# Decode attention with K in one load and the softmax in two parts

## The chip, the cores and the metric

The kernel runs on one core of one Trainium2 chip. The metric is the device time of one execution in microseconds (us). Engines: PE multiplies and transposes, DVE and ACT work element by element, POOL does small copies, SP issues the loads, and 16 DMA engines move the data. SBUF is the on-chip memory that the loads fill; names that start with ps are tiles in PSUM, where PE's results go. QK is K times q, PV is the weights P times V. The granted clock is the share of its full clock that PE was given.

## The reference

One decode step of a transformer block for two sequences. What matters here is the attention: 32 query heads in 4 groups, one K and one V cache per group and sequence (the reference repeats them for the 8 heads of a group).

```python
q = (h @ wq) ...                                    # one token per sequence
scores = einsum('bhqd,bhkd->bhqk', q, k) * Dh ** -0.5   # k: (2, 4, 32768, 128) bf16
p = softmax(scores)
o = einsum('bhqk,bhkd->bhqd', p, v)                 # v as large as k
x = x + ga * (o @ wo);  then an MLP of 1024 -> 3584 -> 1024
```

K and V are 67.1 MB each, the weights 44 MB. Each byte is loaded once.

## The kernel before

There are eight rounds, one for each pair of sequence and KV group. A round has 4 chunks of 8192 rows; a chunk is 8 groups of 8 tiles of 128 rows. SP issues every load on one queue, in order; a load waits until the buffer it overwrites has been read.

```python
def add_k(i, hf):    # two loads of 4 MB: chunks 0-1 and chunks 2-3, 32 KB a partition each
    add(("K", i, hf), [2, TPC * D], A_k_cache[...][hf], hf * 32 * KB, f"K{hf}")
def add_v(i):        # one load of 8 MB, 64 KB a partition
    add(("V", i), [NCH, TPC * D], A_v_cache[...], 64 * KB, "V")
...
for cc in range(NCH):
    for g8 in range(TPC // 8):
        tr(i, cc, g8)                 # PE: 8 transposes of K into PSUM; DVE or ACT copies them out
        pipe.append((i, cc, g8))
        if len(pipe) > PIPE: qk(*pipe.pop(0))     # PE: 8 products with q
        # last qk of a chunk: ACT copies the scores, DVE takes the maximum m1c
while pipe: qk(*pipe.pop(0))
softmax_1(); softmax_2(); softmax_3() # maximum over all 4 chunks and all partitions
for cc in range(NCH): exp(cc)         # DVE subtracts, ACT takes exp
for cc in range(NCH):
    part_sum(cc); pv(i, cc)           # DVE: row sums; PE: P times V into one bank
row_sums(); extract(); extract_2(i)   # the extraction: 1/sum, then the 4 blocks of the bank to "at"
```

## Time and profile before

| | before |
|---|---|
| time, median of 3 runs | 420.08 us (420.07 to 420.27) |
| HBM bytes read | 178.28 MB |
| rounds 1 to 7, from V landed to V landed | 38.61 to 38.71 us |
| busy share PE / DVE / ACT | 70 / 50 / 36 % |
| last load landed, end | 415.76, 418.70 us |

Before one asks what an engine does, one asks in which stretches the DMA is full; the prediction shows that table and the views that go with it. "V landed" means the semaphore event of V's load in the trace.

### The profile page before, as it was taken

The numbers are of one execution on the slowest core, as the hardware profiler recorded it, in microseconds if no ns is written. First come the engines' busy times: TensorE is split into PE (matmuls) and PEld (weight loads), VectorE is DVE, ScalarE is ACT, GpSimd is POOL, SyncE is SP. The second block draws the span as 40 slices with busy tenths as digits, with TensorE's granted clock in tenths as the row PEclk, the third lists the DMA queues.
The fourth block names the chain that finished last, engine by engine and source line by source line (L and its number), as shares of the span: only waits on it lengthen the run. The fifth ranks groups of instructions, "written<-read, shape, count | busy, mean of one in ns | idle before, by whom it ended". The sixth has DMA issues, their size and how long they took to land.

```text
span 418.7 us, 11609 instructions
## 1 busy us (share of the span) xinstructions
PE 291.0 (70%) x5183; PEld 231.3 (55%) x5183; DVE 209.6 (50%) x423; ACT 149.4 (36%) x179; POOL 6.8 (2%) x29
## 2 busy tenths in 40 slices
PE   1407449766996895699369957976995699564536
PEld 1104219762993794299149926962894399221214
DVE  1201105546677676467726664766477567620411
ACT  2000015533565364256405632643365166400100
POOL 3000000000000000000000000000000000000000
PEclk9999557986896997799589958986697889576585
DMA  9989999999999999999999999999999999899995
GB/s 373 450 380 449 448 404 493 398 406 446 441 432 429 423 451 429 419 454 457 391 435 476 407 416 448 438 438 426 438 438 426 416 460 457 377 448 428 424 427 249
DMA packets 5581, 178.42 MB, mean 426 GB/s; under 512 B 698, under 2 KB 706, under 8 KB 964
## 3 DMA queue, kind: packets, MB, share of 16 engines
q1 hardware_dynamic: 5572, 178.28, 98.8%
q8 instruction: 8, 0.13, 0.1%
q14 instruction: 1, 0.01, 0.0%
HBM read 178.28 MB, written 0.00 MB: 426 GB/s over the span
## 4 chain that ended last, share of the span: by engine, by line
DMA 71%; PE 24%; DVE 2%; issue 1%; ACT 1%; SPq 1%
DMA V<-in_A_v_cache_dram 39%; DMA wo<-in_A_wo_dram 10%; DMA K<-in_A_k_cache_dram 10%; PE psZ L584 10%; DMA w<-in_B_w_dram 9%; PE psKT L536 8%; DMA wmod<-in_w_mod_dram 4%; PE psS L548 1%; PE psZ L548 1%; PE psS L655 1%; PE psZ L729 1%; PE psZ L469 1%; ACT KT_sb L540 0%; PE psS L469 0%; DVE m1c L553 0%
## 5 line engine op out<-in xcount | busy, mean ns | idle before, releaser
L536 PE MATMUL psKT<-ident,K 128*128 128x128 bf16 x2048 | 163.1, 229 | 11.5 <-DMA K<-in_A_k_cache_dram 11.5
L540 ACT ACTIVATE KT_sb<-psKT 128x1024 bf16<-128x1024 bf16 x96 | 98.2, 1025 | 124.4 <-PE psKT L536 124.4
L542 DVE COPY KT_sb<-psKT 128x1024 bf16<-128x1024 bf16 x160 | 106.7, 688 | 61.6 <-PE psKT L536 61.2
L536 PEld LDWEIGHTS psKT<-ident,K 128*128 128x128 bf16 x2048 | 126.7, 102 | 13.0 <-DMA K<-in_A_k_cache_dram 12.7
L584 PE MATMUL psZ<-V,E_sb 128*32 128x512 bf16 x512 | 46.4, 541 | 23.2 <-DMA V<-in_A_v_cache_dram 20.0
L548 PE MATMUL psS<-qcur,KT_sb 128*128 128x8 bf16 x1024 | 44.7, 167 | 2.2 <-issue 2.2
L584 PEld LDWEIGHTS psZ<-V,E_sb 128*32 128x32 bf16 x512 | 18.7, 130 | 47.7 <-issue 38.8
L548 PE MATMUL psZ<-qcur,KT_sb 128*128 128x8 bf16 x1024 | 43.0, 167 | 2.2 <-issue 1.5
L548 PEld LDWEIGHTS psS<-qcur,KT_sb 128*128 128x128 bf16 x1024 | 40.0, 97 | 2.3 <-issue 2.3
L548 PEld LDWEIGHTS psZ<-qcur,KT_sb 128*128 128x128 bf16 x1024 | 37.9, 96 | 3.4 <-issue 1.6
L572 ACT ACTIVATE E_sb<-S_sb 128x512 bf16<-128x512 f32 x32 | 19.5, 630 | 29.6 <-DVE S_sb L570 29.6
L570 DVE TENSOR_TENSOR S_sb<-S_sb,gmb 128x512 f32<-128x512 f32 x32 | 20.0, 685 | 0.3
L576 DVE TENSOR_REDUCE rs<-E_sb 128x8 f32<-128x512 bf16 x32 | 19.7, 675 | 0.0
L469 PE MATMUL psS<-wmod,inT 128*32 128x512 bf16 x32 | 5.1, 624 | 16.2 <-DMA wmod<-in_w_mod_dram 16.2
L553 DVE TENSOR_REDUCE m1c<-psZ 128x8 f32<-128x512 f32 x16 | 11.1, 693 | 10.2 <-ACT S_sb L552 10.1
L595 DVE RECIPROCAL rinv<-psM 128x1 f32<-128x1 f32 x8 | 1.3, 168 | 27.7 <-PE psM L593 27.7
L605 PE MATMUL psM<-msum,hmat 128*128 128x128 f32 x16 | 4.2, 347 | 13.3 <-DVE msum L600 13.3
L559 PE MATMUL psM<-identf,m 128*8 128x128 f32 x16 | 4.3, 369 | 13.1 <-DVE m L556 13.1
L553 DVE TENSOR_REDUCE m1c<-psS 128x8 f32<-128x512 f32 x16 | 11.1, 693 | 3.2 <-ACT S_sb L552 3.1
L552 ACT ACTIVATE S_sb<-psZ 128x512 f32<-128x512 f32 x16 | 9.5, 595 | 7.5 <-PE psZ L548 7.5
L477 DVE COPY S_sb<-psS 128x512 f32<-128x512 f32 x1 | 0.7, 690 | 22.9 <-PE psS L469 22.9
L469 PEld LDWEIGHTS psS<-wmod,inT 128*32 128x32 bf16 x32 | 1.1, 132 | 19.3 <-DMA wmod<-in_w_mod_dram 18.0
(123 smaller groups left out, 167.5 us busy)
## 6 DMA issues: line engine op xcount, KB each, us to landing
K<-in_A_k_cache_dram SPq DMA_DIRECT2D x16, 4096.0 KB, 27.1
wq<-in_A_wq_dram SPq DMA_DIRECT2D x2, 4096.0 KB, 44.8
wo<-in_A_wo_dram SPq DMA_DIRECT2D x2, 4096.0 KB, 39.0
w<-in_B_w_dram SPq DMA_DIRECT2D x2, 3584.0 KB, 32.5
wmod<-in_w_mod_dram SPq DMA_DIRECT2D x1, 6144.0 KB, 29.8
w<-in_B_w_dram SPq DMA_DIRECT2D x3, 2048.0 KB, 37.8
wmod<-in_w_mod_dram SPq DMA_DIRECT2D x1, 4608.0 KB, 15.8
wmod<-in_w_mod_dram SPq DMA_DIRECT2D x1, 1536.0 KB, 6.0
```

The costliest lines, as they stand in the source:

```text
L469: pe(lambda e, w=it.view, k=k, kk=kk, ch=ch, n=n, q=q: e.matmul(bank[n][32 * q:32 * q + 32, :], lhsT=inT[:, k, :], rhs=w[:, kk, ch * 512:( ...
L536: pe(lambda e, kq=kq, jj=jj, w=kt, t=t: e.transpose(psKT[kq][:, jj * 128:(jj + 1) * 128], w[:, t, :], ident[:, :]), reads=[it.reg, "ident" ...
L540: act(lambda e, src=src: e.activation(KT_sb[g8][:, :, :], src, ACT.Copy), reads=[f"psKT{kq}"], writes=[f"KT_sb{g8}"], sem=f"ev{cc}_{g8}")
L542: dve(lambda e, src=src: e.tensor_copy(KT_sb[g8][:, :, :], src), reads=[f"psKT{kq}"], writes=[f"KT_sb{g8}"], sem=f"ev{cc}_{g8}")
L548: pe(lambda e, t=t, jj=jj: e.matmul(ps[:, t * HPG:(t + 1) * HPG], lhsT=KT_sb[g8][:, jj, :], rhs=qcur[:, :], start=True, stop=True), reads= ...
L552: act(lambda e: e.activation(Sc, ps.rearrange("p (t h) -> p h t", h=HPG), ACT.Copy), reads=[preg], writes=[f"S_sb_{cc}"], sem=f"sc{cc}")
L553: dve(lambda e: e.tensor_reduce(m1c[:, :, cc], ps.rearrange("p (t h) -> p h t", h=HPG), AX.X, ALU.max), reads=[preg], writes=[f"m1c{cc}"])
L559: pe(lambda e: e.matmul(psM[0:HPG, 0:128], lhsT=m1[:, :], rhs=identf[:, :], start=True, stop=True), reads=["m1", "identf"], writes=["psM"])
L570: dve(lambda e: e.tensor_tensor(Sc, Sc, gmb[:, :].unsqueeze(2).to_broadcast([128, HPG, TPC]), ALU.subtract), reads=[f"S_sb_{cc}", "gmb"], ...
L572: act(lambda e: e.activation(Ec, Sc.rearrange("p h (u t) -> p u h t", t=4), ACT.Exp, scale=SCALE), reads=[f"S_sb_{cc}"], writes=[f"E_sb_{c ...
L576: dve(lambda e: e.tensor_reduce(rs4[:, :, cc], Ec.rearrange("p u h t -> p h u t"), AX.XY, ALU.add), reads=[f"E_sb_{cc}"], writes=[f"rs4_{c ...
L584: pe(lambda e, t4=t4, tg=tg, q=q: e.matmul(psO[32 * q:32 * q + 32, :], lhsT=E_sb[:, tg // 4, :, :].rearrange("p h t -> p (h t)"), rhs=vt[: ...
```

## The change: intent and diff

The change wants PV to end sooner after K, and K to come in packets of 64 KB. Chunks 0 to 2 get their maximum and exponentials while chunk 3 is still being worked on; chunk 3 gets its own maximum, and both parts are weighted with exact factors. K now comes in one load of 8 MB into one buffer. To free that buffer early, DVE copies chunks 2 and 3 into a second 32 KB buffer. The small DVE steps are placed anew, and evacuation of transposed K alternates DVE and ACT.

```diff
-    def add_k(i, hf):
-        add(("K", i, hf), [2, TPC * D], ...[hf], hf * 32 * KB, f"K{hf}")
+    def add_k(i):                       # round 0: two loads ("K", "K2"); others: one
+        add(("K", i), [NCH, TPC * D], rows, 0, "K", view=kv)
...
-        it = need("K", i, cc // 2)
+        it = need("K", i)
+        kt = (kv[:, cc, :] if cc < 2 else kc[:, cc - 2, :])...
-        if EVAC_PATTERN[g8] == "act":   # 5 on DVE, 3 on ACT, the last on DVE
+        if g8 % 2:                      # 4 and 4, the last on ACT
+    def keep(i, n):                     # after groups (0,1), (0,3), (0,5), (1,1)
+        dve(lambda e: e.tensor_copy(kc[:, n // 2, lo:lo + 32 * D], kv[:, 2 + n // 2, lo:lo + 32 * D]), ...)
...
         if g8 == TPC // 8 - 1:
+            dve(... m1c: maximum of the chunk ...)
             act(... scores of the chunk to S_sb ...)
-            dve(... m1c ...)
...
-        softmax_1(); softmax_2(); softmax_3()
-        for cc in range(NCH): exp(cc)
-        for cc in range(NCH): part_sum(cc); pv(i, cc)
-        row_sums(); extract(); extract_2(i)
+        # inside chunk 3: max_1(), max_2(0), max_3(0)
+        exp(0); exp(1); [last qk]; exp(2)
+        pv(i, 0); max_2(1); part_sum(0); pv(i, 1); max_3(1); exp(3); weights()
+        pv(i, 2); part_sum(1); part_sum(2); weights_2(); extract(0)
+        pv(i, 3); part_sum(3); row_sums(); row_sums_2(); extract(1); extract_2(i)
```

(The places of the last weights in the buffers change too.)

More of the change, by code (lines that the diff above doesn't have):

```diff
@@ L34 @@
 RING = 160 * 1024
+KC_AT = 128 * 1024
 AHEAD = ("sc2", "sc3", "pk", "ac")
 WMOD_ITEMS = ((0, 1), (1, 4), (4, 8))
-W2_ITEMS = ((0, 8, 96), (8, 16, 112), (16, 24, 128), (24, 27, 144), (27, 28, 150))
-EVAC_PATTERN = ("dve", "act", "dve", "act", "dve", "dve", "act", "dve")
+W2_ITEMS = ((0, 8, 96), (8, 16, 112), (16, 24, 0), (24, 27, 16), (27, 28, 22))
+KEEP = {(0, 1): 0, (0, 3): 1, (0, 5): 2, (1, 1): 3}
 class Tracker:
@@ L211, in wait @@
             def wait(w):
+                if w[1] == 0:
+                    return eng.wait_ge(self.sem[w[0]], w[2])
                 eng.wait_ge(self.sem[w[0]], val[w[1:]] if w[1:] in val else it * w[1] + w[2])
@@ L250, in bass_adaLN_cond__gqa_block_cached__mixer_channel_mlp__decode_kernel @@
     T = Tracker(nc)
-    T.step["pe"], T.step["dve"] = 72, 14
+    T.step["pe"], T.step["dve"] = 74, 18
     def sb(name, shape, dtype=FP32):
@@ L305, in bass_adaLN_cond__gqa_block_cached__mixer_channel_mlp__decode_kernel @@
     diag = sb("diag", [HPG, HPG])
-    gmb = sb("gmb", [128, HPG])
+    gmb = sb("gmb", [128, 2, HPG])
+    mx = sb("mx", [128, HPG])
+    dw = sb("dw", [128, 2, HPG])
+    wt = sb("wt", [128, 2, HPG])
+    wh = sb("wh", [128, 2, HPG])
+    wp = sb("wp", [128, 2])
+    mkw = sb("mkw", [128, 2, 4])
     rowsum = sb("rowsum", [128, HPG])
-    rs4 = sb("rs4", [128, HPG, NCH])
+    rs4 = sb("rs4", [128, HPG, NCH - 1])
+    rs2 = sb("rs2", [128, 2, HPG])
     rinv = sb("rinv", [128, 1])
@@ L333, in bass_adaLN_cond__gqa_block_cached__mixer_channel_mlp__decode_kernel, with add @@
     KB = 1024
-    def add(key, shape, src, off, slot=None):
+    def add(key, shape, src, off, slot=None, sem=None, view=None):
         it = Item()
@@ L340, in add @@
         it.reg = f"it{it.n}"
-        it.sem = f"d_{slot or it.reg}"
-        it.view = views.get(slot)
+        it.sem = f"d_{sem or slot or it.reg}"
+        it.view = views.get(slot) if view is None else view
         if it.view is None:
@@ L349, in add @@
         by_key[key] = it
-    def add_k(i, hf):
-        add(("K", i, hf), [2, TPC * D], A_k_cache[i % 2, i // 2].rearrange("(p h c t) d -> h p c (t d)", h=2, c=2, p=128)[hf], hf * 32 * KB, f"K{hf}")
+    kv = nc.alloc_sbuf_tensor_at("kv", [128, NCH, TPC * D], BF16, offset=abase)
+    def add_k(i):
+        rows = A_k_cache[i % 2, i // 2].rearrange("(p c t) d -> p c (t d)", c=NCH, p=128)
+        if i:
+            add(("K", i), [NCH, TPC * D], rows, 0, "K", view=kv)
+            by_key["K2", i] = by_key["K", i]
+        else:
+            add(("K", i), [2, TPC * D], rows[:, 0:2, :], 0, sem="K", view=kv[:, 0:2, :])
+            add(("K2", i), [2, TPC * D], rows[:, 2:4, :], 32 * KB, sem="K2", view=kv[:, 2:4, :])
+            T.key("d_K2")
+            T.step["d_K2"] = 0
     def add_v(i):
@@ L364, in bass_adaLN_cond__gqa_block_cached__mixer_channel_mlp__decode_kernel @@
     for i in range(NBG):
-        add_k(i, 0)
-        add_k(i, 1)
+        add_k(i)
         add_v(i)
-    for m, off in enumerate((128, 0)):
+    for m, off in enumerate((0, 32)):
         add(("wo", m), [16, DM], A_wo[m * 2048:(m + 1) * 2048, :].rearrange("(p j) n -> p j n", j=16), off * KB)
     w1_v = B_w1.rearrange("(p k) n -> p k n", k=KT8)
-    for m, off in enumerate((32, 64)):
+    for m, off in enumerate((128, 64)):
         add(("w1", m), [4, F], w1_v[:, 4 * m:4 * m + 4, :], off * KB)
@@ L376, in bass_adaLN_cond__gqa_block_cached__mixer_channel_mlp__decode_kernel @@
     w2_of = {j: (m, j - j0) for m, (j0, j1, off) in enumerate(W2_ITEMS) for j in range(j0, j1)}
+    kc = nc.alloc_sbuf_tensor_at("kc", [128, 2, TPC * D], BF16, offset=abase + KC_AT)
     pos = [0]
@@ L384, in need @@
             old = [o.reg for o in stream[:cur.n] if o.off < cur.off + cur.nbytes and cur.off < o.off + o.nbytes]
+            if cur.n > by_key["V", NBG - 1].n and cur.off < KC_AT + 32 * KB and KC_AT < cur.off + cur.nbytes:
+                old += [f"kc{n}" for n in range(4)]
             if len(cur.view.shape) == 3:
@@ L516, in bass_adaLN_cond__gqa_block_cached__mixer_channel_mlp__decode_kernel @@
                reads=[f"qrow{n}", "ident"] + EREG, writes=["psM"], mark=(i == 3))
-    dve(lambda e: e.tensor_copy(qT[:, :, :], psM[:, 0:64].rearrange("p (b h) -> p b h", b=2)), reads=["psM"], writes=["qT"], sem="mo")
+    dve(lambda e: e.tensor_copy(qT[:, :, :], psM[:, 0:64].rearrange("p (b h) -> p b h", b=2)), reads=["psM"], writes=["qT"], sem="mo1")
     for name in AHEAD:
@@ L521, in bass_adaLN_cond__gqa_block_cached__mixer_channel_mlp__decode_kernel @@
         T.raw("pe", lambda e, name=name: e.sem_inc(T.sem[name], T.step.get(name, 1)))
+    T.wait("dve", writes=[it.reg for it in stream if it.key[0] in ("wmod", "wq")])
     T.wait("pe", reads=["ident", "identf", "onesf", "hmat"], writes=["psS0", "psS1", "psO", "psM"] + [f"psKT{q}" for q in range(NPKT)])
@@ L530, in tr @@
     def tr(i, cc, g8):
-        it = need("K", i, cc // 2)
-        kt = it.view[:, cc % 2, :].rearrange("p (t d) -> p t d", d=D)
+        it = need("K", i)
+        kt = (kv[:, cc, :] if cc < 2 else kc[:, cc - 2, :]).rearrange("p (t d) -> p t d", d=D)
+        k_reg = it.reg if cc < 2 else f"kc{2 * (cc - 2) + g8 // 4}"
         kq = g8 % NPKT
@@ L536, in tr @@
             pe(lambda e, kq=kq, jj=jj, w=kt, t=t: e.transpose(psKT[kq][:, jj * 128:(jj + 1) * 128], w[:, t, :], ident[:, :]),
-               reads=[it.reg, "ident"], writes=[f"psKT{kq}"], mark=(jj == 7))
+               reads=[k_reg, "ident"], writes=[f"psKT{kq}"], mark=(jj == 7))
         src = psKT[kq][:, :].rearrange("p (a n) -> p a n", a=8)
-        if EVAC_PATTERN[g8] == "act":
+        if g8 % 2:
             act(lambda e, src=src: e.activation(KT_sb[g8][:, :, :], src, ACT.Copy), reads=[f"psKT{kq}"], writes=[f"KT_sb{g8}"], sem=f"ev{cc}_{g8}")
@@ L542, in tr @@
             dve(lambda e, src=src: e.tensor_copy(KT_sb[g8][:, :, :], src), reads=[f"psKT{kq}"], writes=[f"KT_sb{g8}"], sem=f"ev{cc}_{g8}")
+    def keep(i, n):
+        it = need("K2", i)
+        lo = n % 2 * 32 * D
+        dve(lambda e: e.tensor_copy(kc[:, n // 2, lo:lo + 32 * D], kv[:, 2 + n // 2, lo:lo + 32 * D]), reads=[it.reg], writes=[f"kc{n}"], sem=f"kc{n}")
     def qk(i, cc, g8):
@@ L551, in qk @@
             Sc = S_sb[:, :, cc * TPC:(cc + 1) * TPC]
+            dve(lambda e: e.tensor_reduce(m1c[:, :, cc], ps.rearrange("p (t h) -> p h t", h=HPG), AX.X, ALU.max), reads=[preg], writes=[f"m1c{cc}"], sem=f"mc{cc}")
             act(lambda e: e.activation(Sc, ps.rearrange("p (t h) -> p h t", h=HPG), ACT.Copy), reads=[preg], writes=[f"S_sb_{cc}"], sem=f"sc{cc}")
-            dve(lambda e: e.tensor_reduce(m1c[:, :, cc], ps.rearrange("p (t h) -> p h t", h=HPG), AX.X, ALU.max), reads=[preg], writes=[f"m1c{cc}"])
@@ L555, in softmax_1 @@
-    def softmax_1():
-        dve(lambda e: e.tensor_reduce(m1[:, :], m1c[:, :, :], AX.X, ALU.max), reads=[f"m1c{cc}" for cc in range(NCH)], writes=["m1"], sem="m1")
-    def softmax_2():
-        pe(lambda e: e.matmul(psM[0:HPG, 0:128], lhsT=m1[:, :], rhs=identf[:, :], start=True, stop=True), reads=["m1", "identf"], writes=["psM"])
-        dve(lambda e: e.tensor_reduce(gm[:, :], psM[0:HPG, 0:128], AX.X, ALU.max), reads=["psM"], writes=["gm"], sem="gm")
-        dve(lambda e: e.tensor_scalar(diag[:, :], identf[0:HPG, 0:HPG], gm[:, 0:1], None, ALU.mult), reads=["identf", "gm"], writes=["diag"], sem="dg")
@@ L563, in softmax_3, with max_1, max_2 @@
-    def softmax_3():
+    def max_1():
+        dve(lambda e: e.tensor_reduce(m1[:, :], m1c[:, :, 0:NCH - 1], AX.X, ALU.max), reads=[f"m1c{cc}" for cc in range(NCH - 1)], writes=["m1"], sem="m1")
+    def max_2(part):
+        src, reg = (m1[:, :], "m1") if part == 0 else (m1c[:, :, NCH - 1], f"m1c{NCH - 1}")
+        pe(lambda e: e.matmul(psM[0:HPG, 0:128], lhsT=src, rhs=identf[:, :], start=True, stop=True), reads=[reg, "identf"], writes=["psM"])
+        dve(lambda e: e.tensor_reduce(gm[:, :], psM[0:HPG, 0:128], AX.X, ALU.max), reads=["psM"], writes=["gm"], sem=f"gm{part}")
+        dve(lambda e: e.tensor_scalar(diag[:, :], identf[0:HPG, 0:HPG], gm[:, 0:1], None, ALU.mult), reads=["identf", "gm"], writes=["diag"], sem=f"dg{part}")
@@ L564, in softmax_3, with max_3 @@
+    def max_3(part):
         pe(lambda e: e.matmul(psM[:, 128:128 + HPG], lhsT=onesf[0:HPG, :], rhs=diag[:, :], start=True, stop=True), reads=["onesf", "diag"], writes=["psM"])
-        dve(lambda e: e.tensor_copy(gmb[:, :], psM[:, 128:128 + HPG]), reads=["psM"], writes=["gmb"])
+        dve(lambda e: e.tensor_copy(gmb[:, part, :], psM[:, 128:128 + HPG]), reads=["psM"], writes=[f"gmb{part}"], sem=f"gb{part}")
     def exp(cc):
+        part = cc // (NCH - 1)
         Sc = S_sb[:, :, cc * TPC:(cc + 1) * TPC]
@@ L569, in exp @@
         Ec = E_sb[:, cc * TPC // 4:(cc + 1) * TPC // 4, :, :]
-        dve(lambda e: e.tensor_tensor(Sc, Sc, gmb[:, :].unsqueeze(2).to_broadcast([128, HPG, TPC]), ALU.subtract),
-            reads=[f"S_sb_{cc}", "gmb"], writes=[f"S_sb_{cc}"], sem=f"sb{cc}")
+        dve(lambda e: e.tensor_tensor(Sc, Sc, gmb[:, part, :].unsqueeze(2).to_broadcast([128, HPG, TPC]), ALU.subtract),
+            reads=[f"S_sb_{cc}", f"gmb{part}"], writes=[f"S_sb_{cc}"], sem=f"sb{cc}")
         act(lambda e: e.activation(Ec, Sc.rearrange("p h (u t) -> p u h t", t=4), ACT.Exp, scale=SCALE), reads=[f"S_sb_{cc}"], writes=[f"E_sb_{cc}"], sem=f"ex{cc}")
@@ L575, in part_sum, with weights, weights_2 @@
         Ec = E_sb[:, cc * TPC // 4:(cc + 1) * TPC // 4, :, :]
-        dve(lambda e: e.tensor_reduce(rs4[:, :, cc], Ec.rearrange("p u h t -> p h u t"), AX.XY, ALU.add), reads=[f"E_sb_{cc}"], writes=[f"rs4_{cc}"])
+        dst, reg = (rs4[:, :, cc], f"rs4_{cc}") if cc < NCH - 1 else (rs2[:, 1, :], "rs2_1")
+        dve(lambda e: e.tensor_reduce(dst, Ec.rearrange("p u h t -> p h u t"), AX.XY, ALU.add), reads=[f"E_sb_{cc}"], writes=[reg])
+    def weights():
+        dve(lambda e: e.tensor_tensor(mx[:, :], gmb[:, 0, :], gmb[:, 1, :], ALU.max), reads=["gmb0", "gmb1"], writes=["mx"])
+        dve(lambda e: e.tensor_tensor(dw[:, :, :], gmb[:, :, :], mx[:, :].unsqueeze(1).to_broadcast([128, 2, HPG]), ALU.subtract), reads=["gmb0", "gmb1", "mx"], writes=["dw"], sem="dw")
+        act(lambda e: e.activation(wt[:, :, :], dw[:, :, :], ACT.Exp, scale=SCALE), reads=["dw"], writes=["wt"], sem="wt")
+    def weights_2():
+        dve(lambda e: e.tensor_tensor(wh[:, :, :], wt[:, :, :], hsel[:, :].unsqueeze(1).to_broadcast([128, 2, HPG]), ALU.mult), reads=["wt", "hsel"], writes=["wh"])
+        dve(lambda e: e.tensor_reduce(wp[:, :], wh[:, :, :], AX.X, ALU.add), reads=["wh"], writes=["wp"])
+        dve(lambda e: e.tensor_tensor(mkw[:, :, :], mk4[:, :].unsqueeze(1).to_broadcast([128, 2, 4]), wp[:, :].unsqueeze(2).to_broadcast([128, 2, 4]), ALU.mult),
+            reads=["mk4", "wp"], writes=["mkw"])
     def pv(i, cc):
@@ L580, in pv @@
         vt = it.view[:, cc, :]
+        last = cc == NCH - 1
+        acc, reg = (psS[0], "psS0") if last else (psO, "psO")
         for t4 in range(TPC // 4):
@@ L583, in pv, with row_sums_2 @@
             q = t4 % 4
-            pe(lambda e, t4=t4, tg=tg, q=q: e.matmul(psO[32 * q:32 * q + 32, :], lhsT=E_sb[:, tg // 4, :, :].rearrange("p h t -> p (h t)"),
+            pe(lambda e, t4=t4, tg=tg, q=q: e.matmul(acc[32 * q:32 * q + 32, :], lhsT=E_sb[:, tg // 4, :, :].rearrange("p h t -> p (h t)"),
                                                     rhs=vt[:, t4 * 512:(t4 + 1) * 512],
-                                                    start=(cc == 0 and t4 < 4), stop=(cc == NCH - 1 and t4 >= TPC // 4 - 4),
+                                                    start=((last or cc == 0) and t4 < 4), stop=(cc >= NCH - 2 and t4 >= TPC // 4 - 4),
                                                     skip_group_check=True),
-               reads=[it.reg, f"E_sb_{cc}"], writes=["psO"], mark=(t4 == TPC // 4 - 1))
+               reads=[it.reg, f"E_sb_{cc}"], writes=[reg], mark=(t4 == TPC // 4 - 1))
     def row_sums():
-        dve(lambda e: e.tensor_reduce(rowsum[:, :], rs4[:, :, :], AX.X, ALU.add), reads=[f"rs4_{cc}" for cc in range(NCH)], writes=["rowsum"])
+        dve(lambda e: e.tensor_reduce(rs2[:, 0, :], rs4[:, :, :], AX.X, ALU.add), reads=[f"rs4_{cc}" for cc in range(NCH - 1)], writes=["rs2_0"])
+        dve(lambda e: e.tensor_tensor(wh[:, :, :], rs2[:, :, :], wt[:, :, :], ALU.mult), reads=["rs2_0", "rs2_1", "wt"], writes=["wh"])
+        dve(lambda e: e.tensor_tensor(rowsum[:, :], wh[:, 0, :], wh[:, 1, :], ALU.add), reads=["wh"], writes=["rowsum"])
         dve(lambda e: e.tensor_copy(rsum16[:, :, :, :], rowsum[:, :].unsqueeze(1).unsqueeze(3).to_broadcast([128, 2, HPG, 8])), reads=["rowsum"], writes=["rsum16"], sem="rs")
+    def row_sums_2():
         pe(lambda e: e.matmul(psM[:, 144:145], lhsT=rsum16.rearrange("p g h e -> p (g h e)"), rhs=onesf[:, 0:1], start=True, stop=True),
@@ L595, in row_sums, with extract @@
         dve(lambda e: e.reciprocal(rinv[:, :], psM[:, 144:145]), reads=["psM"], writes=["rinv"], sem="rv")
-    def extract():
-        dve(lambda e: e.tensor_scalar(msum[:, :], psO[:, 0:128], mk4[:, 0:1], None, ALU.mult), reads=["psO", "mk4"], writes=["msum"])
-        for q in range(1, 4):
-            dve(lambda e, q=q: e.scalar_tensor_tensor(out=msum[:, :], in0=psO[:, q * 128:(q + 1) * 128], scalar=mk4[:, q:q + 1], in1=msum[:, :],
-                                                      op0=ALU.mult, op1=ALU.add), reads=["psO", "mk4", "msum"], writes=["msum"], sem="mo" if q == 3 else None)
+    def extract(part):
+        acc, reg = ((psO, "psO"), (psS[0], "psS0"))[part]
+        for q in range(4):
+            if part == 0 and q == 0:
+                dve(lambda e: e.tensor_scalar(msum[:, :], acc[:, 0:128], mkw[:, 0, 0:1], None, ALU.mult), reads=[reg, "mkw"], writes=["msum"])
+            else:
+                dve(lambda e, q=q: e.scalar_tensor_tensor(out=msum[:, :], in0=acc[:, q * 128:(q + 1) * 128], scalar=mkw[:, part, q:q + 1], in1=msum[:, :],
+                                                          op0=ALU.mult, op1=ALU.add), reads=[reg, "mkw", "msum"], writes=["msum"], sem=f"mo{part}" if q == 3 else None)
     def extract_2(i):
@@ L624, in bass_adaLN_cond__gqa_block_cached__mixer_channel_mlp__decode_kernel @@
                 tr(i, cc, g8)
+                if (cc, g8) in KEEP:
+                    keep(i, KEEP[cc, g8])
                 pipe.append((i, cc, g8))
@@ L629, in bass_adaLN_cond__gqa_block_cached__mixer_channel_mlp__decode_kernel @@
                     qk(*pipe.pop(0))
+                if (cc, g8) == (3, 2):
+                    max_1()
+                if (cc, g8) == (3, 4):
+                    max_2(0)
+                if (cc, g8) == (3, 6):
+                    max_3(0)
+        exp(0)
+        exp(1)
         while pipe:
             qk(*pipe.pop(0))
-        softmax_1()
-        softmax_2()
-        softmax_3()
-        for cc in range(NCH):
-            exp(cc)
-        for cc in range(NCH):
-            part_sum(cc)
-            pv(i, cc)
+        exp(2)
+        pv(i, 0)
+        max_2(1)
+        part_sum(0)
+        pv(i, 1)
+        max_3(1)
+        exp(3)
+        weights()
+        pv(i, 2)
+        part_sum(1)
+        part_sum(2)
+        weights_2()
+        extract(0)
+        pv(i, 3)
+        part_sum(3)
         row_sums()
-        extract()
+        row_sums_2()
+        extract(1)
         extract_2(i)
```

## The prediction

> **What bounds the kernel now.** I started with the stretches of time, because they show at once whether one resource is full everywhere. I cut the span at the moments when the eight V loads land (from the landing events in the trace) and asked for busy time, granted PE clock, DMA share and rate of each stretch:
>
> ```profile
> core 0: us, PE busy (x) PEld busy (x) DVE busy (x) ACT busy (x) POOL busy (x), PEclk, DMA share, GB/s
> 0.00:6.76 6.76, 0.00 (x0) 0.00 (x0) 0.00 (x0) 1.28 (x1) 3.25 (x13) 1.00 0.84 321
> 6.76:62.41 55.65, 24.25 (x213) 11.56 (x213) 7.58 (x27) 4.15 (x6) 0.19 (x1) 0.80 1.00 432
> 130.31:168.97 38.66, 28.86 (x586) 24.52 (x586) 28.11 (x54) 20.62 (x26) 0.44 (x2) 0.85 1.00 434
> 168.97:207.66 38.69, 28.88 (x584) 24.50 (x584) 24.56 (x46) 18.03 (x22) 0.44 (x2) 0.85 1.00 434
> 362.37:413.23 50.86, 27.93 (x269) 13.00 (x269) 12.71 (x46) 3.82 (x7) 0.25 (x1) 0.67 1.00 427
> 413.23:418.70 5.47, 3.16 (x97) 2.81 (x97) 0.68 (x3) 0.00 (x0) 0.00 (x0) 0.50 0.25 100
> ```
>
> The reader should see the last two columns: a DMA share of 1.00 in every stretch between 6.76 and 413.23, at 427 to 434 GB/s, while in one round of 38.69 us PE is busy 28.88, DVE 24.56 and ACT 18.03. Only the first and last few us are not full of DMA. The page's queue lines say the same of the whole:
>
> ```profile
> q1 hardware_dynamic: 5572, 178.28, 98.8%
> HBM read 178.28 MB, written 0.00 MB: 426 GB/s over the span
> ```
>
> Next, the chain that ended last, to see which wait closes a round:
>
> ```profile
> 137.97 31.01 DMA V<-in_A_v_cache_dram
> 168.97 0.14 issue
> 169.11 5.76 PE psZ L584 x62
> 174.92 32.74 DMA V<-in_A_v_cache_dram
> 207.66 0.14 issue
> ```
>
> A round is a V load, then PV (L584), then the next V load. This alternation tempts one to call the PV part of the path: V is issued only when PV has freed its buffer. The sync engine's timeline corrects that:
>
> ```profile
> 150.11 10.67 SPq L389 DMA_DIRECT2D K<-in_A_k_cache_dram  x2
> 174.92 0.33 SPq L389 DMA_DIRECT2D V<-in_A_v_cache_dram  x1
> 188.40 10.68 SPq L389 DMA_DIRECT2D K<-in_A_k_cache_dram  x2
> ```
>
> V, issued at 174.92, lands at 207.66, so it is 32.7 us under way, though 8.39 MB at 434 GB/s need 19.3: it stands 13.4 us in the queue behind K. K, issued at 150.11, starts moving only when V has landed at 168.97, 18.9 us later. So the queue always holds work; PV could end 13 us later before the engines ran dry. And within that round the waits are compute waiting for data:
>
> ```profile
> PE psZ L584 <- DMA V<-in_A_v_cache_dram: 4.1, 1, 4.1
> PE psKT L536 <- DMA K<-in_A_k_cache_dram: 1.3, 1, 1.3
> ```
>
> Conclusion: the bound is the bytes. The rest is 1.75 us until the first packet and 2.9 us from the last landing (415.76) to the end (418.70).
>
> **What the Trainium skill says.** (1) "DMA: Bandwidth & Descriptors", section "Where 436 GB/s comes from": 16 ports give a ceiling of 435.2 GB/s. The trace agrees: 434 in a round. So 178.28 MB need at least 409.7 us; they now take 415.76 - 1.75 = 414.0, and nothing that leaves the bytes alone can win more than 4.3 us, 1.0%. (2) "VectorE: DVE Perf Modes", section "The perf-mode tier table": a bf16 copy within SBUF may run at 4 elements a cycle, from PSUM at 2 at most. The PSUM half is in the trace: the copy of 128x1024 at L542 takes 688 ns; at 0.96 GHz 512 cycles are 533 ns, leaving about 155 of fixed cost. No contiguous SBUF copy of this kind runs in the kernel before, so the 4x is unverified here. (3) "TensorE: Matmul & The Clock Gate", Part 1: PE runs at half clock after an idle time. The trace agrees: a group of eight transposes takes 0.87 us early in a round and 0.47 later, at a granted 0.50 and 1.00.
>
> **The change part by part.**
>
> *K in one 8 MB load.* K packets grow from 32 to 64 KB. In the trace's packet records a 32 KB packet takes 1213 ns, a 64 KB one 2418, so two small ones cost 8 ns more than one large. Seven of eight rounds change: 8 ns x 8 pairs per engine x 7 = 0.45 us at most. But the landings say less: K's 8.39 MB in small packets land 19.31 us after V (188.28 - 168.97), V's in large ones 19.38 us after K. I book -0.2 us.
>
> *Keeping chunks 2 and 3 in a second buffer.* Adds four DVE copies of 128x4096 bf16 a round. Estimate from the skill's 4x and the measured fixed cost: 4096 / 4 / 0.96 GHz = 1067 + 155 = 1.22 us each, 4.9 us a round. DVE goes from 24.6 to roughly 29 of 38.7: more beside the DMA, none on it. Evacuation moves one copy a chunk from DVE (0.69) to ACT (1.03): ACT 18 + 4.1 = 22 us, also free.
>
> *Later start of compute.* This is the price. K used to be usable by halves, the first 9.7 us after V landed; now all of it arrives at 19.3. Reckon from V's landing. Transposes plus QK take 0.47 + 0.18 = 0.65 us a group, 16 groups for chunks 0 and 1: 10.4 us; slow clock at first adds about 4 x 0.4 = 1.6; DVE in chunk 0 has 4 x 0.69 + 0.69 + 3 x 1.22 = 7.1 us of work against PE's 5.2, adding 1.9. The K buffer is free at 19.3 + 10.4 + 1.6 + 1.9 = 33.2. The engines finish the next V at 38.7 and a load needs about 1 us from issue to first packet (0.74 to 1.75 at the start), so K has 4.5 us to spare; it had 18.
>
> *V.* Chunks 2 and 3 add 10.4, to 43.6. From the last QK to PV's end the kernel before took 126.97 + 0.68 to 137.91, about 10.3 us, when V had landed early: 53.9. The split softmax should cut some 4 of that, since chunks 0 to 2 can be multiplied while chunk 3 finds its maximum: about 50. V's turn at the engines comes at 58.0, so the spare is 3 to 7 us. Compute from 19.3 to 54 is 35, below the period of 38.7.
>
> *Round 0.* There K still comes in two loads, landing at 62.4 and 72.3, and the first copy stands early in DVE's order, so DVE waits for 72.3. Copies and evacuations to the end of chunk 1 are 4 x 1.22 + 6 x 0.69 + 0.69 = 9.7 us, so K(1) is issued at 82 to 86 (the latter with the two pauses of 1.5 and 2.2 us that PE shows here at 75.9 and 82.6). V(0)'s packets end at 91.3: in time, by 4 us or more.
>
> *Split softmax, weights, earlier PV extraction.* About ten small DVE operations of 0.17 to 0.35 us, one exp and two matmul steps a round: 2 to 3 us, hidden. In the last round, where a shorter tail could show, PV ends at 368.8 but the output projection waits for its weights, landing at 372.05 and 381.69. So the shortening buys nothing.
>
> *New places for the last weights.* wo now lies in K's buffer: free at about 342.4 + 13.9 = 356, wanted at 361.7. Others have over 10 us. Nothing.
>
> Sum: 420.08 - 0.2 = 419.9.
>
> **The rivals.**
> 1. *The copy runs slower than 4x.* At 2x it takes 2.29 us and K is free at 33.2 + 4 x 1.07 = 37.5, just too late or just in time: 0 to 1 us a round, up to 427. At 1x (4.42 us) it is free at 46, a hole of 8 us in each of seven rounds: about 478. For it: no such copy in the trace. Against: both sides are contiguous bf16 in SBUF.
> 2. *Only round 0 or 1 leaves a hole*, because of the wait for the second half, a cold clock or pauses in instruction fetch: 1 to 4 us once, 421 to 424. For it: the smallest margin is there. Against: I still count 4 us.
> 3. *The gain is real*: larger packets or fewer loads bring the rate up. At best to 435.2 GB/s: 415.7. Against: V in 64 KB packets is no faster today.
> 4. *A shorter softmax shortens each round.* That would be so if PV's end issued a V load that the engines were waiting for, worth some 4 us x 8. Against: the 13 us that V stands in the queue.
>
> **Range and chances.** My case and weak forms of 2 and 3 span 418.8 to 422.0. Two per cent is 8.4 us: faster is excluded by the byte floor (0.01 for what I can't see), slower needs rival 1, or a V chain longer than I count, in every round (0.04). Same: 0.95.
>
> **What would show it.** Right: DMA share 1.00 in every stretch, V landing every 38.6 to 38.7 us, the K copies at about 1.2 us, K issued about 33 us after V landed, and the wait of PE for V gone, replaced by a longer wait for K. The end is again the last weights' landing plus 2.9 us. Wrong: stretches with a DMA share under 0.95, K or V landing in just over 20 us from its issue (an empty queue), copies of 2 us and more, or a rate per round other than 434.

## More of the kernel before

A load's lead is the time from its issue to the landing of the load ahead of it in the queue.

## The result, and the profile after

| | before | after |
|---|---|---|
| time, median of 6 runs | 420.07 us (420.00 to 420.27) | 419.97 us (419.66 to 420.77) |
| V(0) landed to V(7) landed | 270.67 us | 270.52 us |
| last load landed, end | 415.76, 418.70 us | 416.02, 418.96 us |
| busy share PE / DVE / ACT | 70 / 50 / 36 % | 70 / 59 / 43 % |

A ratio here is the mean time of one kernel's fast runs over that of the other's in the same rounds, so not quite the ratio of the medians: 1.0, 95% interval 0.9987 to 1.0013. The change does nothing to the time.

The stretches of the changed kernel, again cut at V's landings (columns as in the prediction):

```profile
6.89:62.32 55.43, 23.31 (x213) 10.76 (x213) 7.59 (x27) 4.15 (x6) 0.19 (x1) 0.72 1.00 433
130.55:169.15 38.60, 30.51 (x613) 26.72 (x611) 29.23 (x60) 22.60 (x27) 0.44 (x2) 0.91 1.00 435
169.15:207.83 38.68, 29.30 (x596) 25.42 (x594) 28.70 (x60) 21.81 (x26) 0.45 (x2) 0.91 1.00 434
362.38:413.60 51.22, 33.79 (x422) 18.93 (x418) 22.98 (x74) 11.14 (x17) 0.25 (x1) 0.73 1.00 427
```

Over the whole kernel DVE has gained 36.5 us of work and ACT 32.4, so 4.6 and 4.0 us a round, and the round has the length it had. The bytes per us are the same.

The chain that ended last in the changed kernel, two of its rounds and its end:

```profile
188.57 3.24 PE psKT L560 x32
...
200.91 26.19 DMA kv<-in_A_k_cache_dram
227.15 3.60 PE psKT L560 x32
...
384.35 29.25 DMA w<-in_B_w_dram
413.65 2.83 PE psZ L799 x96
```

Before, this chain ran through V; now it runs through K, because SP issues K when the transposes of chunk 1 are done (200.91) and PE starts the next round when that K lands (227.1). Of the 26.19 us, 6.9 are waiting in the queue: the bytes need 19.3.

When SP issued the loads:

```profile
162.31 0.33 SPq L411 DMA_DIRECT2D kv<-in_A_k_cache_dram  x1
180.95 0.33 SPq L411 DMA_DIRECT2D V<-in_A_v_cache_dram  x1
200.91 0.33 SPq L411 DMA_DIRECT2D kv<-in_A_k_cache_dram  x1
220.92 0.33 SPq L411 DMA_DIRECT2D V<-in_A_v_cache_dram  x1
```

V landed at 130.55 and 169.15, so K is issued 31.8 us after it, 6.8 and 6.9 ahead of the next landing (169.15 and 207.83). The K that V queues behind landed at 188.53 and 227.11, so V is issued 7.6 and 6.2 us ahead. In the kernel before, these leads were 18.9 and 13.4 us. The same time has been reached with less in reserve.

Last, the copies, and what PE waited for in the round from 169.15 to 207.83:

```profile
L571 DVE COPY kc<-kv 128x4096 bf16<-128x4096 bf16 x32 | 39.0, 1217 | 8.1 <-DMA kv<-in_A_k_cache_dram 8.1
PE psM L642 <- DVE rsum L639: 3.2, 1, 3.2
PEld psKT L560 <- DMA kv<-in_A_k_cache_dram: 1.9, 1, 1.9
```

The wait of PE for V is gone. In its place stands a new wait inside the extraction: PE waits 3.2 us for DVE's row sums. PE's wait for K has not grown: over the whole kernel it was 11.5 us before and is 10.9.

### The profile page after: what moved, and what is told of

Its sections match the earlier page's. It is cut to its first block, busy times and chain, and to the rows that moved or that the text cites. A ratio compares the mean times of both kernels' runs of the same rounds, so it can differ in the third digit from the quotient of the medians.

```text
span 419.0 us, 11898 instructions
## 1 busy us (share of the span) xinstructions
PE 291.7 (70%) x5215; PEld 234.7 (56%) x5215; DVE 246.1 (59%) x535; ACT 181.8 (43%) x219; POOL 6.8 (2%) x29
## 4 chain that ended last, share of the span: by engine, by line
DMA 60%; PE 22%; DVE 9%; issue 5%; ACT 3%; SPq 0%; ACTq 0%; DVEq 0%
DMA kv<-in_A_k_cache_dram 45%; PE psKT L560 13%; DMA wmod<-in_w_mod_dram 7%; DMA w<-in_B_w_dram 7%; ACT KT_sb L564 3%; DVE KT_sb L566 3%; PE psS L577 2%; DVE m1c L581 2%; DVE kc L571 2%; PE psZ L629 1%; PE psZ L577 1%; DVE msum L652 1%; PE psS L725 1%; PE psZ L491 1%; PE psZ L799 1%
## 5 line engine op out<-in xcount | busy, mean ns | idle before, releaser
L564 ACT ACTIVATE KT_sb<-psKT 128x1024 bf16<-128x1024 bf16 x128 | 128.3, 1024 | 96.7 <-PE psKT L560 96.7
L566 DVE COPY KT_sb<-psKT 128x1024 bf16<-128x1024 bf16 x128 | 88.0, 689 | 59.7 <-PE psKT L560 59.4
L560 PE MATMUL psKT<-ident,kv 128*128 128x128 bf16 x1024 | 90.5, 248 | 10.9 <-DMA kv<-in_A_k_cache_dram 10.9
L560 PEld LDWEIGHTS psKT<-ident,kv 128*128 128x128 bf16 x1024 | 73.3, 113 | 12.8 <-DMA kv<-in_A_k_cache_dram 12.8
L560 PE MATMUL psKT<-ident,kc 128*128 128x128 bf16 x1024 | 77.9, 218 | 0.0
L560 PEld LDWEIGHTS psKT<-ident,kc 128*128 128x128 bf16 x1024 | 58.1, 97 | 1.9 <-issue 1.7
L577 PE MATMUL psS<-qcur,KT_sb 128*128 128x8 bf16 x1024 | 45.1, 167 | 10.1 <-DVE KT_sb L566 6.0
L577 PEld LDWEIGHTS psZ<-qcur,KT_sb 128*128 128x128 bf16 x1024 | 36.8, 96 | 13.4 <-ACT KT_sb L564 12.7
L571 DVE COPY kc<-kv 128x4096 bf16<-128x4096 bf16 x32 | 39.0, 1217 | 8.1 <-DMA kv<-in_A_k_cache_dram 8.1
L629 PE MATMUL psZ<-V,E_sb 128*32 128x512 bf16 x384 | 28.3, 414 | 2.0 <-ACT E_sb L603 2.0
L582 ACT ACTIVATE S_sb<-psS 128x512 f32<-128x512 f32 x16 | 9.6, 597 | 20.4 <-DVE m1c L581 20.4
L629 PEld LDWEIGHTS psZ<-V,E_sb 128*32 128x32 bf16 x384 | 11.0, 102 | 9.5 <-ACT E_sb L603 2.7
```

Of the source, the lines that this page charges most:

```text
L560: pe(lambda e, kq=kq, jj=jj, w=kt, t=t: e.transpose(psKT[kq][:, jj * 128:(jj + 1) * 128], w[:, t, :], ident[:, :]), reads=[k_reg, "ident"] ...
L564: act(lambda e, src=src: e.activation(KT_sb[g8][:, :, :], src, ACT.Copy), reads=[f"psKT{kq}"], writes=[f"KT_sb{g8}"], sem=f"ev{cc}_{g8}")
L566: dve(lambda e, src=src: e.tensor_copy(KT_sb[g8][:, :, :], src), reads=[f"psKT{kq}"], writes=[f"KT_sb{g8}"], sem=f"ev{cc}_{g8}")
L571: dve(lambda e: e.tensor_copy(kc[:, n // 2, lo:lo + 32 * D], kv[:, 2 + n // 2, lo:lo + 32 * D]), reads=[it.reg], writes=[f"kc{n}"], sem=f" ...
L577: pe(lambda e, t=t, jj=jj: e.matmul(ps[:, t * HPG:(t + 1) * HPG], lhsT=KT_sb[g8][:, jj, :], rhs=qcur[:, :], start=True, stop=True), reads= ...
L582: act(lambda e: e.activation(Sc, ps.rearrange("p (t h) -> p h t", h=HPG), ACT.Copy), reads=[preg], writes=[f"S_sb_{cc}"], sem=f"sc{cc}")
```

## The experiments

Four questions: do the parts cancel each other, or does neither reach the end (first two runs)? How much reserve is there (no_copy, copy_x2, copy_p2, late_v)? What would the change be worth if the bytes did not bind (five runs with half of V)? And does packet size count (packets_8k)? The kernel before, run beside each group, took 420.04 to 420.19 us.

### The parts alone

**softmax_only**: the changed kernel with K loaded in two halves and transposed straight from them; no copies.

```diff
-        it = need("K", i)
-        kt = (kv[:, cc, :] if cc < 2 else kc[:, cc - 2, :])...
+        it = need("K", i, cc // 2)
+        kt = it.view[:, cc % 2, :]...
-                if (cc, g8) in KEEP:
-                    keep(i, KEEP[cc, g8])
```

> The split softmax and the reordered PV and extraction alone, with K loaded in two halves into two 32 KB buffers as before and no copies. Theory (the bytes set the time: queue never empty): 420 us, within 0.3 us of before; V lands every 38.6 to 38.7 us; PE's waits for V grow. Rival A (the end of PV is on the path, so a shorter softmax shortens each round by some 4 us, and the change lost this again through its later K): 390 to 400 us. Rival B (the parts cancel each other at smaller size): one of the two parts alone faster by over 1 us and the other slower by as much.

Measured: 420.13 us, ratio 0.9998 (0.9982 to 1.0015). The theory holds for the time, and both rivals fall for this part. One sign missed: PE's waits for V were to grow and fell from 20.0 to 8.0 us in all. From round 1 on PE starts each round straight behind the extraction of the last, without waiting for K; so this kernel's compute already fills most of a round.

**kload_only**: the kernel before with the single K load and the copies, the old softmax and the old evacuation pattern.

```diff
-        add_k(i, 0)
-        add_k(i, 1)
+        add_k(i)
...
                 tr(i, cc, g8)
+                if (cc, g8) in KEEP:
+                    keep(i, KEEP[cc, g8])
```

> K in one 8 MB load with 64 KB packets and the four copies alone; softmax, PV and extraction as in the kernel before. Theory: no hole, because K is issued about 33 us after V has landed (turn at 37.6) and PV ends about 54 us after it (turn at 57): 420 to 421 us; the extra us only if round 0 leaves a hole before V(1). Rival A (PV's end on the path): some 9 us a round later than before, about 490 us. Rival B: slower by over 1 us, the mirror image of the softmax alone.

Measured: 423.83 us, ratio 1.0073 (1.0050 to 1.0096): a loss of 3.7 us, under 2% but clear of noise, and more than the theory allowed. Rival A's 490 us is far off. It is no mirror image of the softmax alone, which gains nothing, so rival B falls as well. Yet the parts do act on each other: with the split softmax added, the 3.7 us are gone (419.97), as V is then issued 5.1 to 7.7 us ahead, not 3.7 to 6.4. Two successive rounds of this kernel (columns as before):

```profile
131.44:170.04 38.60, 28.95 (x535) 24.50 (x532) 26.45 (x47) 15.87 (x19) 0.44 (x2) 0.82 1.00 435
170.04:209.68 39.64, 32.50 (x628) 27.89 (x625) 29.38 (x51) 19.20 (x24) 0.45 (x2) 0.83 1.00 427
```

The DMA share says 1.00 in both, and yet the second is 1 us longer at 427 GB/s. The packet records tell why: around 188 us some 64 KB packets took 2.5 to 4.4 us instead of 2.42. A packet that waits still counts as busy. In the short round V was issued at 144.38, 6.4 us before K landed (150.74); in the long one at 185.22, only 4.1 us before (189.35). The same holds in the other rounds: with leads of 5.7 to 6.4 us V landed 19.3 us after K, with 3.7 to 4.4 us it landed 19.7 to 20.4 after. Compute was not the bound here: PE waited for K in each of the seven rounds after the first, 17.1 us in all. So in this kernel leads of under 5 us cost time, where 1 us had been reckoned enough; late_v below shows that 5 is no fixed limit.

### How much reserve there is

**no_copy**: no second buffer; all four chunks are transposed out of the one K buffer.

```diff
-        kt = (kv[:, cc, :] if cc < 2 else kc[:, cc - 2, :])...
+        kt = kv[:, cc, :]...
-                if (cc, g8) in KEEP:
-                    keep(i, KEEP[cc, g8])
```

> The changed kernel without the second K buffer: chunks 2 and 3 are transposed straight out of the single 64 KB buffer, so K is free only after chunk 3. Theory: K is then issued 19.3 + 20.8 + 1.6 = 41.7 us after V landed, past its turn at 37.6; a round lasts 22.4 + 20.7 = 43.1 us instead of 38.7, in six of the seven rounds with a K load that waits: 446 us (440 to 452), DMA share about 0.9 per round. Rival (margins as reckoned are wrong, the queue has slack elsewhere): 420 us.

Measured: 475.9 us, ratio 1.133. The direction is the theory's, the size is not: 56 us instead of 26. Two rounds:

```profile
205.73:252.00 46.27, 31.94 (x588) 27.02 (x588) 24.66 (x55) 21.80 (x26) 0.44 (x2) 0.80 0.85 363
252.00:297.60 45.60, 29.50 (x588) 25.70 (x588) 24.65 (x55) 21.80 (x26) 0.44 (x2) 0.84 0.86 368
```

(These are cut at K's landings.) Here the queue does run empty. Both terms were too small: from K landed to K issued took 23.7 to 24.7 us (expected 22.4), and from issue to landing 21.7 to 21.9 (expected 20.7). The sum is 46.0 us on average, which is the round. And the term that was left out: the last weights also met an empty queue, so that from V(7)'s landing to the last one took 62.5 us, where the changed kernel takes 53.6. So a load into an empty queue costs 2.5 us more than the 19.35 of a queued one. The first packet does start 0.95 us after the issue, as reckoned, but the sixteenth only after 1.7 to 2.0, and nearly all of these first packets take 2.5 to 3.6 us instead of 2.42. Without the copies, then, the single K buffer costs 56 us.

**copy_x2**: each copy is made twice.

```diff
+        dve(lambda e: e.tensor_copy(kc[...], kv[...]), ..., sem=f"kx{n}_0")
         dve(lambda e: e.tensor_copy(kc[...], kv[...]), ..., sem=f"kc{n}")
```

> The changed kernel with each of the four copies made twice: 4.9 us more of DVE work before K is free. Theory: K issued 31.9 + 4.9 = 36.8 us after V landed, still ahead of its turn at 37.6: 420 to 421 us. Rival (a copy's time lies on the path): 8 x 4.9 = 39 us more, 459 us.

Measured: 454.98 us, ratio 1.083. The theory is badly wrong and the rival, which puts each copy's time on the path, nearly right: 35 us for 39 of added copies. K was issued 20 to 23 us after it had landed, not 17.4, because DVE was still at the extraction of the round before when K landed at 114.27; that ended at 120.7. From there on PE never waits for K or V, and the rounds last 41.9 to 43.6 us: the loop of compute that the half-V runs below measure at 37.5, plus 4.9.

**copy_p2**: after the half-V runs below had measured the round of compute, two of the four copies are made twice.

```diff
+        if n % 2:
+            dve(lambda e: e.tensor_copy(kc[...], kv[...]), ..., sem=f"kx{n}")
         dve(lambda e: e.tensor_copy(kc[...], kv[...]), ..., sem=f"kc{n}")
```

> The changed kernel with two of the four copies made twice: 2.4 us more DVE work a round. Theory C (what the doubled copies hit was the compute loop: the changed kernel's whole round of compute, from K's transposes to the end of the extraction, is 37.5 us as its half-V run shows, so 38.7 leaves 1.2 us): 37.5 + 2.4 = 39.9 us a round, some 7 to 8 x 1.2 = 9 us more, 427 to 431 us. Rival D (they hit only the start-up of a K load: K must be issued 2.5 us ahead of its turn): K issued 31.9 + 2.4 = 34.3 us after V landed, in time by 1.8 us: 420 to 421 us.

Measured: 432.95 us, ratio 1.031. Rival D falls. Theory C is right in kind and too small: 13 us against 9, just outside its 427 to 431. From V(0) to V(7) it is 282.6 us, 40.4 a round. K landed at 189.83 in this run, and PE then did this:

```profile
191.51 0.80 PE L659 MATMUL psM<-msum,hmat 128*128 128x128 f32 x2 [1.67 <-DVE msum L654]
192.10 3.19 PE L560 MATMUL psKT<-ident,kv 128*128 128x128 bf16 x28
```

The transposes of the new round start at once behind the old round's extraction, over 2 us after their K had landed. From round 1 on PE waits for no load in this run: the loop of compute is the bound.

**late_v**: V's load also waits for the end of the extraction, so it is issued about 7 us later.

```diff
+            late = ["at"] if cur.key[0] == "V" and cur.key[1] else []
-            T.dma("sp", ..., key=cur.sem, writes=[cur.reg], frees=old)
+            T.dma("sp", ..., key=cur.sem, reads=late, writes=[cur.reg], frees=old)
```

> The changed kernel, but V's load also waits for the end of the extraction of the round before, so it is issued some 7 us later, 57 to 58 us after V landed, just about at its turn. Theory (a load issued less than about 5 us ahead of its turn loses time although no engine shows idle, up to 2.5 us when the queue is empty; the same as lost the K load alone its 3.7 us): 1 to 2 us a round, 428 to 436 us. Rival (what cost the K load alone its time was its compute, not V's late issue): a V that is issued by its turn costs nothing, 420 to 421 us.

Measured: 431.26 us, ratio 1.027 (1.0197 to 1.0332): a loss, though at 2% the verdict is unclear. The rival falls for this kernel: PE waited 2.2 to 2.9 us for K behind the extraction in the long rounds, so compute was not the bound here. Two rounds:

```profile
132.69:171.65 38.96, 28.00 (x540) 24.19 (x538) 27.32 (x57) 20.40 (x25) 0.44 (x2) 0.87 0.99 424
171.65:212.49 40.84, 32.27 (x659) 28.48 (x655) 30.70 (x62) 23.21 (x28) 0.44 (x2) 0.92 0.96 411
```

V issued 0.2 to 0.6 us ahead of K's landing, and 2.0 in the first of these rounds, landed 2.0 to 2.2 us late. But with 2.5 to 2.8 us ahead nothing was lost, where the K load alone had lost 1 us at 4. One difference is visible: after a stall here the engines finish a load within 0.4 to 0.6 us of each other, against 1.7 to 2.5 us in the K load alone, so a queue that runs low meets some engines there much earlier. That this sets the lead needed fits these runs but was not tested by itself.

### With half of V's bytes

V's load brings chunks 0 and 1 only, and PV uses them again for chunks 2 and 3. All compute stays; the result is wrong. (It still passed the comparison with the reference: the attention's part of the output is small, so that comparison says little about V.)

```diff
-        add(("V", i), [NCH, TPC * D], rows, 64 * KB, "V")
+        add(("V", i), [2, TPC * D], rows[:, 0:2, :], 64 * KB, "V")
-        vt = it.view[:, cc, :]
+        vt = it.view[:, cc % 2, :]
```

> The kernel before with half of V's bytes: V's chunks 0 and 1 are loaded, and PV uses them again for chunks 2 and 3, so all compute stays and the result is wrong on purpose. A round then needs 12.6 MB, 29.0 us at 434 GB/s, less than its compute. Theory (bytes): the round falls from 38.7 to what compute needs, by the chain 21 + 5.8 + 5.2 + 2.4 = 34.4 us, and the kernel to about 370 us (360 to 390; the last weights are then partly fetched ahead). Rival (another wait than the bytes, PV's end or a buffer, already set 38.7): no change, 420 us.

> The changed kernel with the same half of V. Its single K buffer makes a loop: K landed, 12.5 us until it is free (measured), 21.9 us from an issue into an empty queue to the landing (measured without the copies): 34.4 us a round. Theory: no better than the kernel before under the same lightening, within 8 us of it, since the shorter softmax is paid for by the K loop. Rival (the shorter softmax is worth some 4 us a round once bytes don't bind): about 30 us faster than the kernel before with half of V.

> The split softmax alone, with half of V. Theory: with K's two halves in separate buffers the K loop is not the limit, and the split softmax and PV order show their worth: 30 to 31 us a round against 34.4, some 25 to 30 us faster than the kernel before with half of V. Rival (the split shortens nothing, its parts being hidden or paid for in the same chain): equal to the kernel before with half of V.

> The single K load with copies alone, with half of V. Theory: slowest of the four; K loop 34.4, and a compute chain from K's landing of 22.5 + 1.9 + 10.3 + 2.4 = 37 us, which starts only when K has landed: 36 to 38 us a round, 10 to 25 us slower than the kernel before with half of V. Rival: equal to it.

Measured, with the phases of a round from the instructions' times in the trace (rounds 2 to 6; "at" is the result of the extraction; the K phase runs from the end of the last round's "at" to the last QK start, "PV" from there to the last PV start, "extraction" from there to the end of "at"; PE starts the new round's transposes 0.8 to 1.0 us ahead of that end):

| with half of V | time, us | K phase | PV | extraction | round |
|---|---|---|---|---|---|
| before | 377.07 | 20.2 | 10.1 to 10.2 | 3.6 | 34.0 |
| softmax alone | 402.17 | 24.2 to 24.8 | 5.1 to 6.6 | 7.3 to 7.5 | 36.6 to 38.9 |
| K load alone | 394.85 | 21.7 | 10.0 to 10.9 | 3.6 | 35.4 to 36.3 |
| both (changed) | 407.65 | 25.0 to 25.1 | 5.1 | 7.3 | 37.4 to 37.5 |

The kernel before falls by 43 us: the bytes were the bound, and its compute needs 34.0 us a round (expected 34.4). The K load alone costs 1.5 us in the K phase (1.9 expected), but is not the slowest. The two kernels with the split softmax come out opposite to what was expected: the split takes up to half off the time from QK to PV's end (10.2 to 5.1 us at best), and yet makes the round longer; the softmax alone takes 25 us more in all than the kernel before. The K loop of 34.4 us that was to bound the changed kernel isn't reached, since its compute takes 37.5.

Where does it go? First into the extraction. PE, end of a round, in the kernel before with half of V:

```profile
204.65 0.39 PE L584 MATMUL psZ<-V,E_sb 128*32 128x512 bf16 x4
204.96 0.38 PE L593 MATMUL psM<-onesf,rsum 128*128 128x1 f32 x2
207.01 0.49 PE L605 MATMUL psM<-msum,hmat 128*128 128x128 f32 x2 [1.67 <-DVE msum L600]
207.46 1.96 PE L536 MATMUL psKT<-ident,K 128*128 128x128 bf16 x32
```

and in the changed one:

```profile
213.39 1.05 PE L629 MATMUL psS<-V,E_sb 128*32 128x512 bf16 x16 [0.67 <-ACT E_sb L603]
217.68 0.38 PE L642 MATMUL psM<-onesf,rsum 128*128 128x1 f32 x2 [3.24 <-DVE rsum L639]
219.73 0.79 PE L657 MATMUL psM<-msum,hmat 128*128 128x128 f32 x2 [1.67 <-DVE msum L652]
220.31 2.98 PE L560 MATMUL psKT<-ident,kv 128*128 128x128 bf16 x26
```

The number in brackets is idle time ahead of the instruction. Before, the row sums were done when PV ended; now PV ends earlier, and the sum over chunk 3, the weights and the first four extraction steps are still to do on DVE, so PE idles 3.24 us more. What was taken out ahead of PV's end now stands behind it. And PE runs the next round's first transposes slowly: 26 in 2.98 us, where 32 took 1.96. Over the first 3.4 us of rounds 2 to 6 the granted clock was 0.50 here and 1.00 before. PE had idled for about 5.5 of the 7.5 us ahead, and for 1.7 before. That this is the cause is not shown: the K load alone with half of V starts every second round at a granted 0.53 to 0.54 after the same 1.7 us.

**pattern_halfv**: the split softmax alone with half of V, but the old evacuation pattern and the old order at a chunk's end.

```diff
-        if g8 % 2:
+        if EVAC_PATTERN[g8] == "act":
...
-            dve(... m1c ...)
             act(... scores ...)
+            dve(... m1c ...)
```

> The split softmax alone with half of V (402 us, 37.6 us a round), but with the evacuation pattern of the kernel before (5 on DVE, 3 on ACT, the last on DVE) and its order at a chunk's end (ACT copies the scores first, then DVE takes the maximum). Theory E (the K phase lost its time at the chunk ends, where ACT must now wait for the maximum, copy the scores and still evacuate the last group): about 2.7 us a round less, 34.5 to 35.2 us, 380 to 386 us. Rival F (the time is lost in the longer extraction after PV, which leaves PE cold): unchanged, 37 us a round and 399 us or more.

Measured: 405.11 us against 402.17. Theory E falls. The K phase did lose 1.3 us or so (23.0 to 23.8 in rounds 2 to 6), but the time from QK to PV's end grew by as much or more (6.8 to 7.6 us), and the extraction stayed at 7.3 to 7.5.

The traces say where the longer K phase comes from. Time in us from a chunk's first transpose to the next chunk's, for chunk 3 to its last QK (rounds 2 to 6):

| with half of V | chunk 0 | 1 | 2 | 3 |
|---|---|---|---|---|
| before | 4.6 | 5.2 | 5.2 | 6.1 |
| softmax alone | 6.5 to 7.0 | 5.7 | 5.7 | 7.4 |
| softmax alone, old pattern | 6.3 to 7.1 | 5.2 | 5.2 | 7.4 |

Chunk 0 is the slow start. Chunks 1 and 2 lose 0.5 us each at a wait of PE for one of ACT's evacuations; the old pattern wins that back. Chunk 3 loses 1.3 us with either pattern, 1.0 to 1.3 of it at the first maximum's matmuls, which now stand between its groups. In the changed kernel, with a wait for ACT again at the end:

```profile
205.05 0.39 PE L589 MATMUL psM<-identf,m 128*8 128x128 f32 x2
206.75 0.38 PE L594 MATMUL psM<-diag,onesf 8*128 8x8 f32 x2
208.80 0.36 PE L577 MATMUL psZ<-qcur,KT_sb 128*128 128x8 bf16 x8 [0.54 <-ACT KT_sb L564]
```

A short round of the softmax alone is so accounted for: 34.0 + 4.3 (the four chunks) + 3.6 (extraction) - 5.1 (PV) - 0.2 (transposes start earlier) = 36.6 us. What stays open is why the clock at its start is lower.

### Packet size

**packets_8k**: the changed kernel, but K and V in eight loads each, so packets of 8 KB.

```diff
-            T.dma("sp", lambda e, ...: e.dma_start(dst, src), ...)
+            # K and V: 8 loads, each an eighth of the row of every partition, one semaphore for all
```

> The changed kernel with every K and V load in eight loads of 8 KB a partition, so packets of 8 KB instead of 64. Theory G (a packet costs 8 ns besides its bytes, as the fit of packet times gave): 128 x 309 ns = 39.6 us a round instead of 38.7, 7 us in all, 427 us. Rival H (the bytes alone count, as the equal landing times of 32 and 64 KB packets suggest): 420 us.

Measured: 424.68 us, ratio 1.011, between the two. The rounds take 39.15 to 39.35 us, from first transpose to first transpose, and a packet 309 ns as expected. 0.58 us a round for 112 more packets an engine is 5.2 ns a packet, not 8: consecutive packets overlap a little (their times sum to 1.01 of the engines' time in such a round). The run changes the number of loads along with the packets, and does not part the two. By this measure K's larger packets are worth 8 x 5.2 ns = 0.04 us a round, 0.3 us in all; 0.15 was seen.

## Why the prediction was right

The time (419.9 against 419.97) and its reason are right. The gain that one might hope for is not lost again elsewhere: the softmax alone takes 420.13. The loss that one might fear is partly held off, though: the K load alone takes 423.83.

- **The bound is the bytes: right.** Rate and DMA share are the same before and after, and taking 33.6 MB away shortens the kernel before by 43 us. (The byte floor of 409.7 us is an estimate from the ceiling that the prediction cites; no stretch shown here went above 435 GB/s.)
- **Packets, -0.2 us: in keeping.** V(0) to V(7) shrank by 0.15 us, in one profile of each kernel; in the softmax alone, with 32 KB packets, it did not shrink (270.67). In the total, 0.2 us is below the noise.
- **Copies of 1.22 us: right** (1.217), so rival 1, a slow copy, did not arise. Nor did rival 2: K(1) landed 19.30 us after V(0), with no hole.
- **K and V in time: right.** K issued 31.7 to 32.8 us after V landed (33.2 predicted), PV ended after 50.3 to 51.8 (about 50), K(1) was issued at 83.0 (82 to 86), wo at 356.1 (356).
- **The waits: half right.** PE's wait for V is gone, but no longer wait for K took its place (11.5 to 10.9 us in all); the wait for row sums did.
- **The end: right.** Last landing 416.02 plus 2.94 us.
- **The reserve: wrong, and harmless only because both parts came together.** Three terms were mis-sized. "A load needs about 1 us from issue to first packet": the first packet starts after 0.95 us, but a start from empty costs 2.5 us, and leads of 3.7 to 4.4 us cost up to 1.1 us in the K load alone. There PV ended 52.6 to 54.0 us after V had landed, where the prediction saw 3 us to spare at 54, and time was lost; with the split softmax it ended early enough. "Compute from 19.3 to 54 is 35" left out the extraction, behind which the next round's transposes stand on PE: it is 37.5, 1.2 us short of the period and not 3.7. And "at 2x ... up to 427" was built on these: adding 2.4 us of copies gave 433, adding 4.9 gave 455, and copies at 2x would have added 4.3.
- **"The split softmax should cut some 4": right as far as it goes** (5.1 between QK and PV's end), but it is only half of the account. The extraction grew by 3.7 us and the K phase by 4.0 to 4.9. The prediction had put the added steps at "2 to 3 us, hidden"; they are hidden only because the bytes take longer.

So PV's end was not on the path of the kernel before, and shortening it alone could win nothing. What the change really altered is the reserve. The kernel before could compute a round in 34.0 us, the changed one needs 37.5 of the 38.7 that the bytes give it.

## What to carry to other kernels

Where each load stands in the queue well before its turn (here 5 us or more), a shorter wait for a buffer buys nothing; look at how long it stands there before calling its issue the path. A DMA share of 1.00 alone does not say that the lead is enough. Then measure the reserve by taking bytes away: it shows what the compute really needs, and whether a change that costs nothing today has spent that reserve. Count a round up to the point where the next one can start, not up to the event that frees the next buffer.

## What the Trainium skill lacked or had wrong

- "DMA: Bandwidth & Descriptors", section "Latency and other measured facts", gives about 600 ns to the first byte for loads issued from SP, without saying from when. Here the first packet started 0.95 us after the issue began and 0.62 to 0.64 after it ended, so the two agree if the end is meant. The section puts most of a load's fixed cost of about 2 us down to the receipt at its end. It doesn't say that the first packets after an empty queue are slow: 2.5 to 3.6 us instead of 2.42 for 64 KB; an 8.39 MB load took 21.7 to 21.9 us from its issue instead of 19.35.
- "Perfetto Trace Analysis", section "Identifying the Most-Contended Engine", calls the occupancy of the DMA engines misleading, and names as the reason that there are 16 of them. The runs agree and add another: a round with a DMA share of 1.00 ran at 427 GB/s and lost 1 us, because packets that took 2.5 to 4.4 us instead of 2.42 count as busy throughout.
- "VectorE: DVE Perf Modes", section "The perf-mode tier table", has the 4x copy within SBUF at 2048 elements alone (693 ns). It holds at another size: 1217 ns for 4096 bf16 a partition, that is 1067 ns at 4x and 150 of fixed cost.
- No page says how early a load must be issued to keep the rate: in the K load alone 5.7 us ahead lost nothing and 3.7 to 4.4 us lost up to 1.1 us; in late_v 2.5 us ahead lost nothing and 2.0 lost 2.2.
